# Attention with a gated MLP behind it on one core: the last 64 keys scored by four 64x64 fp32 products from the unsplit loads, and the attention's bursts aligned with pairs of units

## The chip, the cores and the metric

The kernel runs on one core of a Trainium2 chip. Its time is what the device reports for an execution, in microseconds (us), as the median over the runs. The engines are TensorE (PE for its matmuls, PEld for its weight loads), VectorE (DVE), ScalarE (ACT), GpSimd (POOL) and SyncE (SP), which here issues every transfer. Each engine runs its own instructions in the order of the program and waits for the others by semaphores.

## The reference

Eight batches, twelve heads, 448 positions, head width 64. Attention with a sigmoid in place of the softmax, and behind it a gated MLP in which the gate half is normalized and mixed over the positions:

```
scores = q @ k.T / sqrt(64) - log(448)
attn   = 1 / (1 + exp(-scores))
x      = heads side by side of (attn @ v)          # 8 x 448 x 768
h      = relu(x @ w_in);  u, g = halves of h       # 512 wide each
g      = (g - mean) / sqrt(var + 1e-6)             # over the 512
out    = (u * (w_spatial @ g + b_spatial)) @ w_out
```

Everything is fp32. Products run in two ways. In the **split** form both operands are cut in two fp32r parts, a high one (a rounded copy) and a low one (the rest), and three products are added: high-high, low-high, high-low (`TERMS`). In the **direct** form TensorE is given fp32 operands as they are; the trace then shows two matmul instructions for each.

## The kernel before

The work goes in four stages of two batches. A stage has attention for its two batches and then the MLP: `gate_values` (pv), `spatial` (pg), `gated` (pu), `output` (po). The MLP is not touched. A **unit** is two heads of one batch; its queries and keys lie in one load `raw`, 128 partitions by 896 columns, the two heads on partitions 0 to 63 and 64 to 127. Units are taken in pairs, six pairs to a stage, 24 in all.

448 keys are three tiles of 128 and a rest of 64. A pair of units makes seven score tiles (`TILES`): tiles 0 to 2 are the full ones of the first unit, tile 3 (`NFULL`) holds the last 64 keys of both units, one in the upper and one in the lower half of the partitions, tiles 4 to 6 are the full ones of the second unit.

- `attention_loads` (line 195) brings a unit's queries and keys, `value_loads` the values of a pair. Weight loads of the first stage share the buffers tagged `raw`, of which there are three.
- `attention_splits` (line 205) makes the two fp32r parts `qks` of a unit: a copy (ACT in the first stage, DVE later) and a subtraction on DVE (lines 99 and 100). A memset (line 212) puts 64 columns of zeros beside them. The keys of the first unit end with the 64-key rest and then the zeros; for the second unit the zeros and the rest stand in front. So a stationary operand of 128 columns, 64 of them zeros, can add one unit's rest to one half of tile 3.
- `attention_scores` (line 223): a full tile is three terms for each of two heads, six matmuls with 64 rows and 128 columns; the two heads use two row halves of TensorE and run at once. Tile 3 is twice that, twelve matmuls, six for each unit. The scores land in one of three two-bank buffers (`psc`); ACT turns them into `at` by the sigmoid (line 242), of which there are seven buffers.
- `attention_values` (line 247) multiplies `at` by the values, in direct fp32. A full tile is two products of 128 rows and 64 columns, one for each head, beside each other in TensorE's columns. Tile 3 is four products of 64 rows and 64 columns, in the four quadrants. The sums of a unit gather in one of two banks (`pav`), and when a unit is complete they are split into `x_s` (ACT copies, DVE subtracts).

The order on TensorE is the order of the program. The attention's tiles stand in one list, taken in **bursts of four** whatever unit they belong to: four score tiles, then the value products of the four before (`BURST`, lines 405 to 447). Loads and splits are issued from inside this loop, by the number of the tile. In the first stage, conversion of the weights (`load_weights`, mostly DVE work) runs between the tiles, one step for nearly every tile. The scores of the first three tiles of each later stage are put ahead of the last output products of the stage before.

Of the kernel before, what the change touches and what calls it, by code (L numbers as in the profile page):

```python
# [8 lines left out]
F32 = mybir.dt.float32  # L9
F32R = mybir.dt.float32r  # L10
U32 = mybir.dt.uint32
# [3 lines left out]
P = 128  # L15
# [20 lines left out]
def attn_gmlp_kernel(  # L36
# [25 lines left out]
    nc = tc.nc  # L62
    B, NHP, _, _ = qk.shape
    S = out.shape[3]
    D = P // 2
# [4 lines left out]
    HALF = 64  # L70
    NFULL = 3

    PART = 2 * S + HALF
    QK = 1.0 / math.sqrt(D)
    NEG_LOG_S = -math.log(S)
    NT = 2 * S // P
# [2 lines left out]
    work = ctx.enter_context(tc.tile_pool(name="work", bufs=2))  # L79
# [18 lines left out]
    def split(hi, lo, src, copy):  # L98
        copy(hi, src)  # L99
        nc.vector.tensor_sub(lo, src, hi.bitcast(F32))  # L100

    def banks(name):
        return ps_2.tile([P, 2, 512], F32, tag="ps2", name=name)
# [35 lines left out]
    def weight_steps():  # L139

        steps = []
        for i in range(NCC):
            steps += [(w_in, w_in_s, NCC + i)] + [(w_sp, w_sp_s, i)] * (i < NFC)
        steps += [(w_in, w_in_s, i) for i in range(NCC)]
        steps += [(w_out, w_out_s, i) for i in range(NFC * DM // 512)]
        raws = {}

        def load(n):
            if n < len(steps):
                src, _, i = steps[n]  # L150
                w = 512 if src is w_sp else 1024

                if n < NFIRST:
                    raw = work.tile([P, 1024], U32, tag="tmp", name=f"wraw_{n}", bufs=3)[:, :w]
                else:
                    raw = work.tile([P, 1024], U32, tag="raw", name=f"wraw_{n}", bufs=3)
                raws[n] = raw.bitcast(F32) if src is w_sp else raw
                nc.sync.dma_start(raws[n], src[:, i * w : (i + 1) * w])

        for n in range(AHEAD):  # L160
            load(n)
        for n, (src, dst, i) in enumerate(steps):
            load(n + AHEAD)
            if src is w_sp and i == 0:
                nc.sync.dma_start(b_bc, b_sp.broadcast_to([P, 512]))
            hi, lo = dst[:, i, 0], dst[:, i, 1]
            scalar = n >= NFIRST
            val = raws.pop(n)
            if src is not w_sp:
                raw = val  # L170
                val = work.tile([P, 512], U32, tag="wval", name=f"wval_{n}", bufs=2)
                yield from convert(val, raw, scalar)
                val = val.bitcast(F32)
            if scalar:
                nc.scalar.copy(hi, val)
                yield
            else:
                nc.vector.tensor_copy(hi, val)
            nc.vector.tensor_sub(lo, val, hi.bitcast(F32))
            if not scalar:  # L180
                yield


    NFIRST = NCC + NFC + 3

    weights = weight_steps()

    def load_weights(n):
        for _ in range(n):
            next(weights, None)  # L190

    loaded = {}
    values = {}

    def attention_loads(b, hp):
        raw = work.tile([P, 1024], F32, tag="raw", name=f"raw_{b}_{hp}", bufs=3)[:, : 2 * S]
        nc.sync.dma_start(raw, qk[b, hp])
        loaded[b, hp] = raw

    def value_loads(b, hp):  # L200
        vt = work.tile([P, 2 * NFULL + 1, P], F32, tag="v", name=f"v_{b}_{hp}", bufs=3)
        nc.sync.dma_start(vt, v[b, hp // 2])
        values[b, hp] = vt

    def attention_splits(b, hp):
        raw = loaded[b, hp]
        s = work.tile([P, 2, PART], F32R, tag="split", name=f"qks_{b}_{hp}", bufs=3)


        odd = hp % 2  # L210
        zeros = s[:, :, :HALF] if odd else s[:, :, 2 * S :]
        nc.vector.memset(zeros.bitcast(F32), 0.0)
        body = s[:, :, HALF:] if odd else s[:, :, : 2 * S]

        split(body[:, 0], body[:, 1], raw, nc.vector.tensor_copy if b > 1 else nc.scalar.copy)
        loaded[b, hp] = s

    TERMS = ((0, 0), (1, 0), (0, 1))


    TILES = 2 * NFULL + 1

    def attention_scores(b, hp, t):
        psc = banks(f"psc_{b}_{hp}_{t}")
        parts = []
        for odd in range(2):
            if t == NFULL or (t > NFULL) == odd:
                full = 2 * HALF if odd else 0
                k = (0 if odd else 2 * S - HALF) if t == NFULL else full + t % (NFULL + 1) * P
                parts += [(loaded[b, hp + odd], k, full + NFULL * P, a, e) for a, e in TERMS]  # L230
        for i, (s, k, q, a, e) in enumerate(parts):
            for j in range(2):
                rows = slice(j * D, (j + 1) * D)
                nc.tensor.matmul(  # L234
                    psc[:, j, :S],
                    s[rows, a, k : k + P],
                    s[rows, e, q : q + S],
                    start=i == 0,
                    stop=i == len(parts) - 1,
                )  # L240
        at = work.tile([P, 2, 512], F32, tag="big", name=f"at_{b}_{hp}_{t}", bufs=7)[:, :, :S]
        nc.scalar.activation(at, psc[:, :, :S], AF.Sigmoid, bias=bias_s, scale=QK)  # L242
        return at
# [3 lines left out]
    def attention_values(b, hp, t, at):  # L247
        vt = values[b, hp]
        for odd in range(2):
            if t == NFULL:  # L250
                rows = slice(odd * HALF, (odd + 1) * HALF)
            elif (t > NFULL) == odd:
                rows = slice(0, P)
            else:
                continue
            unit = b, hp + odd
            start = t == odd * NFULL
            stop = t == (1 + odd) * NFULL
            if start:
                pav_of[unit] = ps_1.tile([P, 512], F32, tag="ps1", name=f"pav_{b}_{hp + odd}")  # L260
            pav = pav_of[unit]
            for j in range(2):
                heads = slice(j * D, (j + 1) * D)
                nc.tensor.matmul(pav[heads, :S], vt[rows, t, heads], at[rows, j], start=start, stop=stop)  # L264
# [140 lines left out]
    BURST = 4  # L405
    units = [(b, hp) for b in range(B) for hp in range(NHP)]

    def ahead(f, n):
        if n < len(units):
            f(*units[n])  # L410

    def start_loads(m):
        n = m * 2 * NHP
        ahead(attention_loads, n)
        ahead(value_loads, n)
        ahead(attention_loads, n + 1)
        ahead(attention_loads, n + 2)

    def attention(m):

        first, end = 2 * NHP * m, 2 * NHP * (m + 1)
        tiles = [(n, t) for n in range(first, end, 2) for t in range(TILES)]
        before = []

        for i in range(-1, len(tiles) + BURST, BURST):
            now = []
            for n, t in tiles[max(i, 0) : i + BURST]:
                if n == first and t < 2:
                    ahead(attention_splits, n + t)
                if n + 2 < end:  # L430
                    if t == 0:
                        ahead(attention_loads, n + 3)
                        ahead(value_loads, n + 2)
                    elif t == NFULL and n + 4 < end:
                        ahead(attention_loads, n + 4)

                    elif t in (2, 5):
                        ahead(attention_splits, n + 2 + t // 5)
                now.append((*units[n], t, attention_scores(*units[n], t)))

                if m == 0 and i >= BURST - 1 and t != 2:
                    load_weights(1)
            yield
            for args in before:
                attention_values(*args)
            before = now
            yield
# [88 lines left out]
```

## Time and profile before

| what | value |
|---|---|
| median of 3 runs | 712.94 us (712.74 to 713.23) |
| profiled execution, first to last instruction | 711.3 us (the profile gives no other time of it) |
| PE busy | 696.7 us, 98% |
| DVE busy | 290.9 us, 41% |
| ACT busy | 256.2 us, 36% |
| score matmuls (line 234) | 1152, busy 137.3 us |
| value matmuls (line 264) | 768, busy 140.8 us |
| sigmoids (line 242) | 168, 1.007 us each |
| granted TensorE clock | 1.00 throughout |

How to read the views: a row of the timeline has the start and the length in us, the engine, the line, the operation, output<-inputs, the shapes and the number of instructions merged into the row; in brackets stands how long the engine was idle before it and what ended that. Shapes such as 64*128 are rows by columns of TensorE. A row of the groups has busy us and mean ns of one behind the bar, then the idle time before. A matmul's end is modelled, so durations of single matmuls overlap; the distance between the starts of two bursts is the safer measure. A row of the windows view has the stretch, its length, then the busy time and instruction count of PE, PEld, DVE, ACT and POOL, the granted clock, the share of time that the DMA engines were busy, and GB/s.

### The profile page before, as it was taken

How to read it: one execution, taken by the hardware profiler on the slowest of the kernel's cores; microseconds unless marked ns; L12 is line 12 of the kernel's file. 1: busy time of each engine (PE TensorE's matmuls, PEld its weight loads, DVE VectorE, ACT ScalarE, POOL GpSimd, SP SyncE). 2: the span in 40 equal slices, each digit the busy share in tenths (PEclk: the TensorE clock that was granted, in tenths of full speed). 3: DMA queues.
4: the chain of work that ended last, by engine and by line, in shares of the span. 5: the costliest groups of instructions: out<-in, count | busy, mean ns of one | idle time of the engine just before them, and what ended most of it. 6: DMA issues, size and time to landing. Idle time of an engine off the chain costs nothing.

```text
span 711.3 us, 9237 instructions
## 1 busy us (share of the span) xinstructions
PE 696.7 (98%) x3928; PEld 521.4 (73%) x3928; DVE 290.9 (41%) x494; ACT 256.2 (36%) x304; POOL 18.5 (3%) x36
## 2 busy tenths in 40 slices
PE   6999999999999999999999999999999999999997
PEld 4455688888755568999865548899986555889996
DVE  3999288723334226320234413722125331462110
ACT  6787221322477611001357661101136664101111
POOL 0000001000000001000000000100000000110000
PEclk9999999999999999999999999999999999999999
DMA  7773002320633200002253220000125310000102
GB/s 254 260 267 114 30 30 80 117 105 0 214 124 130 78 1 0 1 1 78 76 183 116 93 78 1 0 1 27 52 100 186 104 53 1 1 0 1 53 26 79
DMA packets 20249, 55.39 MB, mean 78 GB/s; under 512 B 1904, under 2 KB 8048, under 8 KB 20208
## 3 DMA queue, kind: packets, MB, share of 16 engines
q1 hardware_dynamic: 20208, 54.80, 22.6%
q8 instruction: 31, 0.51, 0.3%
q14 instruction: 10, 0.08, 0.0%
HBM read 43.78 MB, written 11.01 MB: 77 GB/s over the span
## 4 chain that ended last, share of the span: by engine, by line
PE 85%; DVE 9%; ACT 2%; issue 1%; DMA 1%; POOL 1%; SPq 0%; ACTq 0%
PE pav L264 19%; PE psc L234 17%; PE po L275 15%; PE pu L275 14%; PE pv L275 13%; PE pg L275 8%; DVE wval L128 1%; DVE g L374 1%; DVE vn L316 1%; ACT gs L99 1%; DVE wval L131 1%; ACT wraw L121 1%; DVE gs L100 1%; DMA wraw<-w_in_dram 1%; DVE stats L299 1%
## 5 line engine op out<-in xcount | busy, mean ns | idle before, releaser
L242 ACT ACTIVATE at<-psc,bias_s 128x896 f32<-128x896 f32 x168 | 160.3, 1007 | 53.9 <-PE psc L234 43.3
L234 PE MATMUL psc<-qks 64*128 64x448 f32 x1152 | 137.3, 379 | 6.0 <-ACT qks L99 4.8
L264 PE MATMUL pav<-at,v 128*64 128x448 f32 (+1 forms) x768 | 140.8, 552 | 0.7 <-DVE x_s L100 0.7
L234 PEld LDWEIGHTS psc<-qks 64*128 64x128 f32 x1152 | 104.2, 187 | 50.2 <-ACT x_s L99 17.6
L275 PE MATMUL po<-gs,w_out_s 128*128 128x448 f32 x576 | 122.1, 369 | 2.5 <-DVE gs L100 1.6
L275 PE MATMUL pu<-x_s,w_in_s 128*128 128x448 f32 x576 | 118.2, 365 | 1.0 <-DVE g L352 1.0
L275 PEld LDWEIGHTS po<-gs,w_out_s 128*128 128x128 f32 x576 | 107.2, 188 | 15.9 <-DVE gs L100 3.5
L275 PE MATMUL pv<-w_in_s,x_s 128*128 128x512 f32 x504 | 115.4, 390 | 0.0
L275 PEld LDWEIGHTS pu<-x_s,w_in_s 128*128 128x128 f32 x576 | 108.1, 188 | 9.9 <-DVE g L352 1.3
L275 PEld LDWEIGHTS pv<-w_in_s,x_s 128*128 128x128 f32 x504 | 94.3, 188 | 22.3 <-issue 2.8
L264 PEld LDWEIGHTS pav<-at,v 128*64 128x64 f32 (+1 forms) x768 | 41.7, 135 | 81.2 <-issue 79.1
L100 DVE TENSOR_TENSOR x_s<-pav,x_s 128x448 fp32r<-128x448 f32 x48 | 29.8, 623 | 115.6 <-ACT x_s L99 115.6
L275 PE MATMUL pg<-w_sp_s,vn 128*128 128x448 f32 x352 | 72.8, 365 | 0.0
L275 PEld LDWEIGHTS pg<-w_sp_s,vn 128*128 128x128 f32 x352 | 66.0, 187 | 5.8
L374 DVE SCALAR_TENSOR_TENSOR g<-pu,g 128x896 f32<-128x896 f32 x16 | 17.5, 1091 | 126.2 <-PE pu L275 126.2
L402 ACT COPY osb<-po 128x896 f32<-128x896 f32 x24 | 21.8, 907 | 113.0 <-PE po L275 113.0
L99 ACT CAST gs<-g 128x896 fp32r<-128x896 f32 x16 | 15.1, 943 | 129.8 <-DVE g L374 129.8
L100 DVE TENSOR_TENSOR qks<-raw,qks 128x896 fp32r<-128x896 f32 x48 | 51.9, 1081 | 8.4 <-ACT qks L99 7.2
L295 ACT ACTIVATE rv<-pv 128x1024 f32<-128x1024 f32 (+1 forms) x16 | 14.6, 914 | 83.5 <-PE pv L275 83.5
L299 DVE BATCH_NORM_STATS2 stats<-rv 128x6 f32<-128x512 f32 x28 | 19.0, 679 | 44.9 <-ACT rv L295 44.9
L99 ACT CAST x_s<-pav 128x448 fp32r<-128x448 f32 x48 | 25.5, 530 | 29.5 <-PE pav L264 29.5
L352 DVE TENSOR_TENSOR g<-pg,b_bc 128x896 f32<-128x896 f32 x16 | 17.4, 1088 | 20.0 <-PE pg L275 20.0
(32 smaller groups left out, 210.6 us busy)
## 6 DMA issues: line engine op xcount, KB each, us to landing
raw<-qk_dram SPq DMA_DIRECT2D x48, 448.0 KB, 4.1
v<-v_dram SPq DMA_DIRECT2D x24, 448.0 KB, 3.9
out_dram<-osb SPq DMA_DIRECT2D x24, 448.0 KB, 2.6
wraw<-w_in_dram SPq DMA_DIRECT2D x12, 512.0 KB, 4.3
wraw<-w_out_dram SPq DMA_DIRECT2D x6, 512.0 KB, 3.6
wraw<-w_sp_dram SPq DMA_DIRECT2D x4, 256.0 KB, 4.5
b_bc<-b_sp_dram SPq DMA_DIRECT2D x1, 256.0 KB, 4.7
```

The costliest lines, as they stand in the source:

```text
L99: copy(hi, src)
L100: nc.vector.tensor_sub(lo, src, hi.bitcast(F32))
L121: nc.scalar.mul(af, af, 2.0**-112)
L234: nc.tensor.matmul(psc[:, j, :S], s[rows, a, k : k + P], s[rows, e, q : q + S], start=i == 0, stop=i == len(parts) - 1,)
L242: nc.scalar.activation(at, psc[:, :, :S], AF.Sigmoid, bias=bias_s, scale=QK)
L264: nc.tensor.matmul(pav[heads, :S], vt[rows, t, heads], at[rows, j], start=start, stop=stop)
L275: nc.tensor.matmul(ps, st, mv, start=start and i == 0, stop=stop and i == len(ops) - 1)
L295: nc.scalar.activation(rv[:, :n], pv[:, :n], AF.Relu)
L299: nc.vector.bn_stats(stats, rv[:, i])
L352: nc.vector.tensor_add(g, pg[:, :, :S], bb)
L374: nc.vector.scalar_tensor_tensor(g, pu[:, :, :S], 0.0, g, op0=ALU.max, op1=ALU.mult)
L402: nc.scalar.copy(osb, po[:, :, :S])
```

## The change

Tile 3's scores are no longer made from the split parts. Four fp32 products with 64 rows and 64 columns read the keys' rest and the queries straight from `raw`, for two units and two heads, each in its own quadrant of TensorE. The zeros and their memset go, `qks` holds 832 columns in place of 896 (the rest's keys are not split), and the host lays out both units alike. `raw` stays in use until tile 3's scores, and has four buffers instead of three; `wval`, a buffer of the weights' conversion, has one instead of two. The order of loads at a stage's start becomes unit, unit, values, unit.

The order of the attention is written out by pairs of units: scores of tiles 0 to 2 and tile 3, values of the last four tiles of the pair before, scores of tiles 4 to 6, values of tiles 0 to 2. The second unit's split is now issued at tile 1 of its own pair, the next pair's first split at tile 4.

```diff
-    PART = 2 * S + HALF
+    REST = NFULL * P
+    PART = REST + S
...
-        zeros = s[:, :, :HALF] if odd else s[:, :, 2 * S :]
-        nc.vector.memset(zeros.bitcast(F32), 0.0)
-        body = s[:, :, HALF:] if odd else s[:, :, : 2 * S]
-
-        split(body[:, 0], body[:, 1], raw, nc.vector.tensor_copy if b > 1 else nc.scalar.copy)
-        loaded[b, hp] = s
+        split(s[:, 0], s[:, 1], raw[:, :PART], nc.vector.tensor_copy if b > 1 else nc.scalar.copy)
+        parts_of[b, hp] = s
...
+        heads = [slice(j * D, (j + 1) * D) for j in range(2)]
+        if t == NFULL:
+            for odd in range(2):
+                raw = loaded[b, hp + odd]
+                for j, rows in enumerate(heads):
+                    nc.tensor.matmul(
+                        psc[odd * HALF : (odd + 1) * HALF, j, :S],
+                        raw[rows, PART : PART + HALF],
+                        raw[rows, REST:PART],
+                        start=True,
+                        stop=True,
+                    )
+        else:
+            s = parts_of[b, hp + t // (NFULL + 1)]
+            k = t % (NFULL + 1) * P
+            for i, (a, e) in enumerate(TERMS):
+                for j, rows in enumerate(heads):
+                    nc.tensor.matmul(
+                        psc[:, j, :S],
+                        s[rows, a, k : k + P],
+                        s[rows, e, REST:PART],
+                        start=i == 0,
+                        stop=i == len(TERMS) - 1,
+                    )
...
+        def scores(n, tiles):
+            for t in tiles:
+                if t == 1 or n == first and t == 0:
                     ahead(attention_splits, n + t)
+                if n + 2 < end and t == NFULL + 1:
+                    ahead(attention_splits, n + 2)
+                waiting.append((*units[n], t, attention_scores(*units[n], t)))
                 if n + 2 < end:
                     if t == 0:
                         ahead(attention_loads, n + 3)
                         ahead(value_loads, n + 2)
                     elif t == NFULL and n + 4 < end:
                         ahead(attention_loads, n + 4)
...
+        for n in range(first, end, 2):
+            scores(n, range(NFULL))
+            if n == first:
+                yield
+            scores(n, [NFULL])
+            if n > first:
+                sums(NFULL + 1)
+            scores(n, range(NFULL + 1, TILES))
+            sums(NFULL)
+        sums(NFULL + 1)
```

`sums(k)` issues the value products of the k oldest tiles that wait for them.

TensorE's order around the third pair of the first batch, before. In the names, `psc_4_1` and `at_4_1` are tile 1 of the pair that begins with unit 4, `qks_4` and `raw_4` belong to unit 4, `pav_4` is its sum, `v_4` its values; the last number only counts buffers.

```order
L234 MATMUL psc_4_0_327<-qks_4_233 128x448 x6
L264 MATMUL pav_2_338<-at_2_0_214,v_2_92 64x448 x2
L264 MATMUL pav_2_338<-at_2_1_229,v_2_92 64x448 x2
L264 MATMUL pav_2_338<-at_2_2_244,v_2_92 64x448 x2
L264 MATMUL pav_2_338<-at_2_3_261,v_2_92 64x448 x2
L264 MATMUL pav_3_347<-at_2_3_261,v_2_92 64x448 x2
L234 MATMUL psc_4_1_352<-qks_4_233 128x448 x6
L234 MATMUL psc_4_2_369<-qks_4_233 128x448 x6
L234 MATMUL psc_4_3_380<-qks_4_233 128x448 x6
L234 MATMUL psc_4_3_380<-qks_5_293 128x448 x6
L234 MATMUL psc_4_4_401<-qks_5_293 128x448 x6
L264 MATMUL pav_3_347<-at_2_4_287,v_2_92 64x448 x2
```

The same place with the change:

```order
L239 MATMUL psc_4_0_305<-qks_4_256 128x448 x6
L239 MATMUL psc_4_1_323<-qks_4_256 128x448 x6
L239 MATMUL psc_4_2_336<-qks_4_256 128x448 x6
L227 MATMUL psc_4_3_345<-raw_4_130 64x448 x2
L227 MATMUL psc_4_3_345<-raw_5_197 64x448 x2
L269 MATMUL pav_2_298<-at_2_3_235,v_2_100 64x448 x2
L269 MATMUL pav_3_362<-at_2_3_235,v_2_100 64x448 x2
L269 MATMUL pav_3_362<-at_2_4_266,v_2_100 64x448 x2
L269 MATMUL pav_3_362<-at_2_5_279,v_2_100 64x448 x2
L269 MATMUL pav_3_362<-at_2_6_294,v_2_100 64x448 x2
L239 MATMUL psc_4_4_378<-qks_5_320 128x448 x6
L239 MATMUL psc_4_5_389<-qks_5_320 128x448 x6
```

The 64-key scores stand directly before the 64-key values of the pair before; a burst no longer cuts through a pair.

VectorE's order at the start of the program, before (`wraw` and `wval` belong to the first weight's conversion):

```order
L212 MEMSET qks_0_86 128x2x64
L100 TENSOR_TENSOR qks_0_86<-raw_0_78,qks_0_86 128x896
L212 MEMSET qks_1_103 128x2x64
L100 TENSOR_TENSOR qks_1_103<-raw_1_82,qks_1_103 128x896
L212 MEMSET qks_2_116 128x2x64
L100 TENSOR_TENSOR qks_2_116<-raw_2_84,qks_2_116 128x896
L112 TENSOR_SCALAR wval_152<-wraw_146 128x512
L123 TENSOR_SCALAR wraw_146<-wraw_146 128x512
L126 TENSOR_SCALAR wraw_146<-wraw_146 128x512
L128 SCALAR_TENSOR_TENSOR wval_152<-wraw_146,wval_152 128x512
```

And with the change:

```order
L101 TENSOR_TENSOR qks_0_86<-raw_0_78,qks_0_86 128x832
L101 TENSOR_TENSOR qks_1_102<-raw_1_80,qks_1_102 128x832
L113 TENSOR_SCALAR wval_138<-wraw_132 128x512
L124 TENSOR_SCALAR wraw_132<-wraw_132 128x512
L127 TENSOR_SCALAR wraw_132<-wraw_132 128x512
L101 TENSOR_TENSOR qks_2_142<-raw_2_84,qks_2_142 128x832
L129 SCALAR_TENSOR_TENSOR wval_138<-wraw_132,wval_138 128x512
```

The third unit's split has moved behind the first three instructions of the weight's conversion. On SP the order of these loads stays: raw_4, then the first weight.

More of the change, by code (lines that the diff above doesn't have):

```diff
@@ L155, in load @@
                 else:
-                    raw = work.tile([P, 1024], U32, tag="raw", name=f"wraw_{n}", bufs=3)
+                    raw = work.tile([P, 1024], U32, tag="raw", name=f"wraw_{n}", bufs=4)
                 raws[n] = raw.bitcast(F32) if src is w_sp else raw
@@ L170, in weight_steps @@
                 raw = val
-                val = work.tile([P, 512], U32, tag="wval", name=f"wval_{n}", bufs=2)
+                val = work.tile([P, 512], U32, tag="wval", name=f"wval_{n}", bufs=1)
                 yield from convert(val, raw, scalar)
@@ L195, in attention_loads @@
     def attention_loads(b, hp):
-        raw = work.tile([P, 1024], F32, tag="raw", name=f"raw_{b}_{hp}", bufs=3)[:, : 2 * S]
+        raw = work.tile([P, 1024], F32, tag="raw", name=f"raw_{b}_{hp}", bufs=4)[:, : 2 * S]
         nc.sync.dma_start(raw, qk[b, hp])
@@ L203, in value_loads @@
         values[b, hp] = vt
+    parts_of = {}
     def attention_splits(b, hp):
@@ L207, in attention_splits @@
         s = work.tile([P, 2, PART], F32R, tag="split", name=f"qks_{b}_{hp}", bufs=3)
-        odd = hp % 2
-        zeros = s[:, :, :HALF] if odd else s[:, :, 2 * S :]
-        nc.vector.memset(zeros.bitcast(F32), 0.0)
-        body = s[:, :, HALF:] if odd else s[:, :, : 2 * S]
-        split(body[:, 0], body[:, 1], raw, nc.vector.tensor_copy if b > 1 else nc.scalar.copy)
-        loaded[b, hp] = s
+        split(s[:, 0], s[:, 1], raw[:, :PART], nc.vector.tensor_copy if b > 1 else nc.scalar.copy)
+        parts_of[b, hp] = s
     TERMS = ((0, 0), (1, 0), (0, 1))
@@ L224, in attention_scores @@
         psc = banks(f"psc_{b}_{hp}_{t}")
[L225 to L240, printed above, removed]
+        heads = [slice(j * D, (j + 1) * D) for j in range(2)]
[22 more added lines that the diff above has]
+                    )
         at = work.tile([P, 2, 512], F32, tag="big", name=f"at_{b}_{hp}_{t}", bufs=7)[:, :, :S]
@@ L403, in output @@
         nc.sync.dma_start(out[b, es[0] : es[0] + 2].rearrange("e p s -> p e s"), osb)
-    BURST = 4
     units = [(b, hp) for b in range(B) for hp in range(NHP)]
@@ L414, in start_loads @@
         ahead(attention_loads, n)
+        ahead(attention_loads, n + 1)
         ahead(value_loads, n)
-        ahead(attention_loads, n + 1)
         ahead(attention_loads, n + 2)
@@ L421, in attention @@
         first, end = 2 * NHP * m, 2 * NHP * (m + 1)
[L422 to L428, printed above, removed]
+        waiting = []
+        def scores(n, tiles):
+            for t in tiles:
+                if t == 1 or n == first and t == 0:
                     ahead(attention_splits, n + t)
+                if n + 2 < end and t == NFULL + 1:
+                    ahead(attention_splits, n + 2)
+                waiting.append((*units[n], t, attention_scores(*units[n], t)))
                 if n + 2 < end:
@@ L435, in attention, with sums @@
                         ahead(attention_loads, n + 4)
[L437 to L441, printed above, removed]
+                if m == 0 and (n > first or t >= NFULL) and t != 2:
                     load_weights(1)
-            yield
-            for args in before:
+        def sums(n):
+            for args in waiting[:n]:
                 attention_values(*args)
-            before = now
-            yield
+            del waiting[:n]
+        for n in range(first, end, 2):
[8 more added lines that the diff above has]
+        sums(NFULL + 1)
     start_loads(0)
@@ L499 @@
     qk = np.concatenate([full, q, short], axis=2)
-    qk[:, 2::4] = np.concatenate([short, full, q], axis=2)[:, 2::4]
-    qk[:, 3::4] = np.concatenate([short, full, q], axis=2)[:, 3::4]
     qk = np.ascontiguousarray(np.transpose(qk, (0, 1, 3, 2))).reshape(B, H // 2, 2 * D, 2 * S)
```

## The prediction

> **What bounds the kernel now.** I read the page first: busy shares and the chain that ended last.
>
> ```profile
> span 711.3 us, 9237 instructions
> PE 696.7 (98%) x3928; PEld 521.4 (73%) x3928; DVE 290.9 (41%) x494; ACT 256.2 (36%) x304; POOL 18.5 (3%) x36
> PE 85%; DVE 9%; ACT 2%; issue 1%; DMA 1%; POOL 1%; SPq 0%; ACTq 0%
> PE pav L264 19%; PE psc L234 17%; PE po L275 15%; PE pu L275 14%; PE pv L275 13%; PE pg L275 8%; DVE wval L128 1%; DVE g L374 1%; DVE vn L316 1%; ACT gs L99 1%; DVE wval L131 1%; ACT wraw L121 1%; DVE gs L100 1%; DMA wraw<-w_in_dram 1%; DVE stats L299 1%
> ```
>
> TensorE sets the end. Lines 234 (scores) and 264 (values), which the change touches, hold 36% of the chain. A shorter PE stream there shortens the run, unless something else takes over. Next, the timeline of PE through the attention of the second stage (start, length, then the burst):
>
> ```profile
> 188.05 3.50 PE L234 MATMUL psc<-qks 64*128 64x448 f32 x30
> 191.48 2.48 PE L264 MATMUL pav<-at,v 128*64 128x448 f32 x12
> 193.88 3.54 PE L234 MATMUL psc<-qks 64*128 64x448 f32 x30
> 197.36 3.39 PE L264 MATMUL pav<-at,v 64*64 64x448 f32 x20
> ...
> 238.90 3.52 PE L234 MATMUL psc<-qks 64*128 64x448 f32 x30
> 242.35 3.39 PE L264 MATMUL pav<-at,v 64*64 64x448 f32 x20
> 245.67 2.08 PE L234 MATMUL psc<-qks 64*128 64x448 f32 x18
> 247.68 5.79 PE L264 MATMUL pav<-at,v 128*64 128x448 f32 x32
> 253.41 16.84 PE L275 MATMUL pv<-w_in_s,x_s 128*128 128x512 f32 x73
> ```
>
> Distances between starts are what the bursts cost. Three value tiles take 193.88 - 191.48 = 2.40 us; the last seven, with the 64-key tile among them, 253.41 - 247.68 = 5.73. With a for a value tile (four instructions, or eight 64x64 ones) and c for a change of tile shape, 3a + c = 2.40 and 7a + 3c = 5.73 are both met by a = 0.75, c = 0.16. A burst of three score tiles (18 matmuls, nine concurrent pairs) takes 247.68 - 245.67 = 2.01: less c, 1.85, or 0.206 per pair. Closer, one burst of each kind:
>
> ```profile
> 225.96 2.92 PE L234 MATMUL psc<-qks 64*128 64x448 f32 x24
> 226.94 3.95 ACT L242 ACTIVATE at<-psc,bias_s 128x896 f32<-128x896 f32 x4 [1.63 <-PE psc L234]
> ...
> 228.00 0.50 PEld L234 LDWEIGHTS psc<-qks 64*128 64x128 f32 x6 [0.33 <-ACT at L242]
> ...
> 228.80 3.54 PE L264 MATMUL pav<-at,v 128*64 128x448 f32 x20
> 229.71 0.21 PEld L264 LDWEIGHTS pav<-at,v 64*64 64x64 f32 x8 [0.70 <-issue]
> 230.62 0.20 PEld L264 LDWEIGHTS pav<-at,v 128*64 128x64 f32 x4 [0.71 <-issue]
> ```
>
> Two things. The 64-key value tile holds PE for 230.62 - 229.71 = 0.91 = a + c: four fp32 64x64 products cost one a. And the fourth score tile of a burst begins at 228.00, 2.04 after the burst, where three tiles need 1.85: it waits for the first tile's sigmoid, since there are three score buffers. Four pairs of units, in the windows view (us, then PE, PEld, DVE, ACT busy):
>
> ```profile
> 193.88:238.90 45.02, 45.02 (x322) 24.00 (x320) 18.16 (x31) 30.64 (x36) 0.00 (x0) 1.00 0.36 121
> ```
>
> 45.02 / 4 = 11.26 us per pair of units. Built from the pieces: 24 concurrent score pairs x 0.206 = 4.93, seven value tiles x 0.75 = 5.25, five changes of shape x 0.16 = 0.80, together 10.98; the remaining 0.28 are stalls on that fourth tile. ACT is busy 30.64 and DVE 18.16 of 45.02, so neither is near here, and the granted clock is 1.00.
>
> **The change in the steady pairs.** It removes twelve matmuls (six concurrent pairs) per pair of units: 6 x 0.206 = -1.23. It adds four fp32 64x64 products. No row has these operands; the nearest is the value tile of the same shape, and I take its a = +0.75. Each row group writes a bank of its own in both cases. Below 0.75 nothing speaks: all four quadrants are used already. Above it stand 1.50 (two at a time) and 3.0 (one after another), treated as rivals. Shape changes stay five: scores, 64x64, values, scores, values, scores, because the 64-key scores stand directly before the previous pair's 64-key values. Bursts of three need no fourth buffer, so the 0.28 goes; but the 64-key scores are a fourth tile behind three. They can begin 2.04 after the burst's start and would without a wait at 1.85 + 0.16 = 2.01, so the wait is 0.03 if the change of shape runs beside it and up to 0.2 if it comes after. I take 0.1. A steady pair is then 18 x 0.206 + 0.75 + 5.25 + 0.80 + 0.1 = 10.60 against 11.26.
>
> Stages two to four, from 188.05 to 253.41 = 65.36 before: first pair 0.91 + 2.01 + 2.40 = 5.3 (its first three tiles were scored earlier, as now), five pairs of 10.60 = 53.0, last four value tiles 4 x 0.75 + 2 x 0.16 = 3.3. Sum 61.6, gain 3.7 a stage (4.2 with no wait, 3.1 with 0.22), three stages 11.1 (9.3 to 12.6).
>
> **Edits that I cost at nothing.** In these stages ACT has 14 us of 45 free and DVE 27, which covers the splits moved to tiles 1 and 4: the second needs a copy and a subtraction behind the sums' last x_s, and PE reads it three score and three value tiles later, 2.01 + 2.41 = 4.4 us.
>
> ```profile
> L99 DVE CAST qks<-raw 128x896 fp32r<-128x896 f32 x36 | 20.5, 569 | 5.4 <-DMA raw<-qk_dram 5.4
> ```
>
> With the subtraction's 1.03 and an x_s of 0.62 (both rows below) that is 2.2 behind ACT's copy of the sums: over 1 us to spare, and only what exceeds 4.4 would cost. The raw loads now wait for the 64-key product instead of the split.
>
> ```profile
> raw<-qk_dram SPq DMA_DIRECT2D x48, 448.0 KB, 4.1
> ```
>
> A load issued behind the product of pair n is split a full pair later, over 10 us on, against 4.1. The single wval buffer adds no wait: on DVE the next conversion already stands behind the subtraction of the last, which needs ACT's copy of it. Removed memsets cost PE nothing here.
>
> **The first stage** differs: weights are converted between the tiles.
>
> ```profile
> 20.00:30.00 10.00, 9.31 (x66) 4.05 (x64) 9.73 (x20) 6.96 (x9) 0.00 (x0) 1.00 0.80 258
> ...
> 40.00:50.00 10.00, 10.00 (x72) 4.97 (x70) 9.69 (x20) 7.94 (x10) 0.00 (x0) 1.00 0.95 332
> ```
>
> DVE is busy 97% there: 10.9 us of each 11.26. Its groups in 20 to 60 us:
>
> ```profile
> L100 DVE TENSOR_TENSOR qks<-raw,qks 128x896 fp32r<-128x896 f32 x7 | 7.2, 1028 | 0.0
> L179 DVE TENSOR_TENSOR w_in_s<-wval,w_in_s 128x512 fp32r<-128x512 f32 x7 | 4.8, 693 | 0.2
> L100 DVE TENSOR_TENSOR x_s<-pav,x_s 128x448 fp32r<-128x448 f32 x7 | 4.2, 616 | 0.0
> L131 DVE SCALAR_TENSOR_TENSOR wval<-wraw,wval 128x512 uint32<-128x512 uint32 x6 | 4.2, 692 | 0.2
> L126 DVE TENSOR_SCALAR wraw<-wraw 128x512 f32<-128x512 f32 x7 | 3.1, 437 | 0.2
> L178 DVE CAST w_in_s<-wval 128x512 fp32r<-128x512 f32 x6 | 2.5, 418 | 0.0
> L212 DVE MEMSET qks<- 128x128 f32 x7 | 1.2, 165 | 0.0
> ```
>
> Per pair of units two memsets go (0.33), and two subtractions shrink from 896 to 832 columns (2 x 0.07): DVE needs 10.4, PE 10.6. DVE just keeps up, with no room. And at the start it now has the third split behind the first weight's conversion:
>
> ```profile
> 7.09 1.01 ACT L242 ACTIVATE at<-psc,bias_s 128x896 f32<-128x896 f32 x1 [2.34 <-PE psc L234]
> 7.99 0.93 ACT L99 CAST qks<-raw 128x896 fp32r<-128x896 f32 x1
> ...
> 10.07 0.33 SPq L197 DMA_DIRECT2D raw<-qk_dram  x1
> 10.44 0.43 SPq L158 DMA_DIRECT2D wraw<-w_in_dram  x1
> ...
> 15.49 0.43 DVE L112 TENSOR_SCALAR wval<-wraw 128x512 uint32<-128x512 uint32 x1 [3.71 <-DMA wraw<-w_in_dram]
> ...
> 26.98 3.39 PE L264 MATMUL pav<-at,v 128*64 128x448 f32 x20 [0.69 <-DVE x_s L100]
> ```
>
> The fifth raw load, ahead of the weight on SP, now waits for the first 64-key product. That product needs the first sigmoid's buffer (7.09 + 1.01 = 8.1) and 0.9 more, so the two loads are issued at 9.2 and 9.6; with the 5.05 us from 10.44 to 15.49 the weight is there at 14.65. Three conversions (3 x 0.44) and the subtraction (1.03 for 896 columns in the rows above, so 0.96 for 832) end at 17.0. PE has run out by then: the seventh score tile needs the buffer of the fourth sigmoid, so behind the first one a split copy (0.9) and three sigmoids (3.95 for four, above: 0.96 apart) to 11.9; it ends at 12.5 and three value tiles at 14.9. PE stands for 2.1 us. From 17.0: 2.01 + 0.75 + 3.32 end the first four-tile sums at 23.1 and three score tiles at 25.1. DVE meanwhile does 2 x 0.69 + 0.42 + 0.69 (weight), 0.42 + 0.69 (spatial weight), 3 x 0.44, a subtraction of 0.96, and 2 x 0.69 + 0.42 + 0.69 again: 8.4, to 25.4, then x_s 0.62, to 26.0. The next value product needs the bank that this frees: 0.9 more of a stall. From 26.0: 2.41 + 4 x 10.60 + 3.32 = 74.1.
>
> ```profile
> 76.90 28.86 PE L275 MATMUL pv<-w_in_s,x_s 128*128 128x512 f32 x126
> ```
>
> The first stage's attention ended at 76.90, so it gains 2.8; nothing if DVE falls behind, 4.2 as elsewhere if the weight lands early enough. The rest of each stage stays as it is.
>
> **Sum:** 11.1 + 2.8 = 13.9, from the profiled span of 711.3 to 697.4. The median of the runs, 712.94, lies 1.6 above that span (launch and end, unchanged): 699.0.
>
> **Rivals.** *VectorE takes the first stage.* For it: 97% busy, and in-order waits on x_s with weight work behind them. Against: its work falls by 0.48 per pair, PE's by 0.66. Then that stage gains nothing: 712.94 - 11.1 = 701.8, and 703.6 with the long wait at the 64-key tile.
>
> *The four quadrants share out badly: slower.* The four score products come in another order than the value products: both units' row groups first, then the second column group. If the latter two wait for the first two, the tile costs 1.50, every pair of units 0.75 more, 24 x 0.75 = 18.0 - 13.9: 4.1 slower, 717.0. One after another, 3.0 and 24 x 2.25 - 13.9 = 40 slower, 753. It decides above 0.75 + 13.9 / 24 = 1.33 us for the tile. Against it, in the windows view, the value tile that began at 65.84:
>
> ```profile
> 65.94:66.04 0.10, 0.10 (x4) 0.10 (x8) 1.00 0.00 0
> ```
>
> Four matmuls run at once, and eight weight loads beside them. [...]
>
> *The loads come late*, since raw buffers are held longer: a load would have to take over 10 us instead of 4.1 to 5.05; I give it no case of its own.
>
> **How the numbers follow.** Forecast 0.70, VectorE in the first stage 0.19, the quadrants 0.07 (two turns 0.05, four 0.02), something better than 695.5 or not thought of 0.04. The forecast's own ends are 12.6 + 4.2 (696.1) and 9.3 + 2.8 (700.8); the range goes on through the first rival: 695.5 to 704. A measurement tells about 0.2%, 1.4 us, from no change: faster 0.92, the same 0.02, slower 0.06.
>
> **What would show it.** Right: PE's bursts in stages two to four start 10.5 to 10.7 us apart per pair; the 64x64 scores and the 64x64 values behind them hold PE 1.6 to 1.9 together; no three-tile burst waits on ACT; in the first stage PE waits for the split of the third unit near 15 to 17 us, and its attention ends near 74. Wrong: a 64-key score tile of 1.5 us or more, waits of PE on DVE in each pair of the first stage, or waits on raw loads.

## The result, and the profile after

The changed kernel takes 700.76 us (four runs, 699.55 to 700.91) against 712.84 (712.70 to 713.23): ratio 0.9825, 95% interval 0.9811 to 0.9839, 12 us less. The prediction was 699.0 in a range of 695.5 to 704. Two runs of the experiments below, of 964.88 and 1726.77 us, lie far outside all others and are left out of their medians. The page of the profile after:

```profile
span 699.1 us, 9084 instructions
PE 683.1 (98%) x3832; PEld 504.5 (72%) x3832; DVE 283.2 (41%) x446; ACT 253.9 (36%) x304; POOL 18.5 (3%) x36
PE 87%; DVE 7%; ACT 2%; issue 2%; DMA 1%; POOL 1%; SPq 0%; ACTq 0%
```

TensorE still sets the end. Its timeline through the second stage's attention:

```profile
187.59 0.98 PE L227 MATMUL psc<-raw 64*64 64x448 f32 x8
188.50 2.11 PE L239 MATMUL psc<-qks 64*128 64x448 f32 x18
190.54 2.48 PE L269 MATMUL pav<-at,v 128*64 128x448 f32 x12
192.95 2.09 PE L239 MATMUL psc<-qks 64*128 64x448 f32 x18
194.99 0.98 PE L227 MATMUL psc<-raw 64*64 64x448 f32 x8
195.79 3.34 PE L269 MATMUL pav<-at,v 64*64 64x448 f32 x20
199.06 2.09 PE L239 MATMUL psc<-qks 64*128 64x448 f32 x18
...
203.48 2.09 PE L239 MATMUL psc<-qks 64*128 64x448 f32 x18
...
243.21 5.79 PE L269 MATMUL pav<-at,v 128*64 128x448 f32 x32
248.94 11.41 PE L280 MATMUL pv<-w_in_s,x_s 128*128 128x512 f32 x49
```

The 64-key scores hold PE for 195.79 - 194.99 = 0.80 us, with no change of shape to the 64x64 values behind them. A pair of units takes 203.48 - 192.95 = 10.53 (11.26 before), the stretch 248.94 - 187.59 = 61.35 (65.36). Stages three and four give 61.63 (418.88 - 357.25) and 61.34 (588.53 - 527.19), where the kernel before has 65.34 in both, so the three stages gained 11.7 together.

The first stage is different. PE's timeline, and then the windows view of the same time (the granted clock is the third number from the end):

```profile
9.12 1.77 PE L227 MATMUL psc<-raw 64*64 64x448 f32 x8
10.82 2.25 PE L239 MATMUL psc<-qks 64*128 64x448 f32 x18
...
15.40 0.47 PE L239 MATMUL psc<-qks 64*128 64x448 f32 x2
17.93 3.36 PE L239 MATMUL psc<-qks 64*128 64x448 f32 x16 [2.06 <-DVE qks L101]
21.21 1.03 PE L227 MATMUL psc<-raw 64*64 64x448 f32 x8
...
75.21 28.88 PE L280 MATMUL pv<-w_in_s,x_s 128*128 128x512 f32 x126
```

```profile
16.00:18.00 2.00, 0.07 (x2) 0.07 (x2) 1.93 (x5) 0.00 (x0) 0.00 (x0) 0.99 0.51 209
18.00:20.00 2.00, 2.00 (x12) 1.80 (x14) 1.90 (x4) 0.85 (x1) 0.00 (x0) 0.50 0.00 0
20.00:21.00 1.00, 1.00 (x8) 0.63 (x4) 0.96 (x3) 1.00 (x3) 0.00 (x0) 0.50 0.74 244
21.00:22.00 1.00, 1.00 (x10) 0.40 (x12) 0.97 (x3) 1.00 (x2) 0.00 (x0) 0.82 0.54 174
```

PE idled 2.06 us for the third unit's split, as predicted. Unpredicted is what came behind: the clock was granted at 0.50, and the sixteen score matmuls from 17.93 to 21.21 took 3.28 us. The attention ended at 75.21 against 76.90, 1.7 less. And the first stage's MLP got longer, from 76.90 to the next scores at 175.95 before (99.05), from 75.21 to 175.49 now (100.28). Its two waits of PE, before and after:

```profile
123.10 7.57 PE L275 MATMUL pu<-x_s,w_in_s 128*128 128x448 f32 x36 [0.98 <-DVE g L352]
...
145.72 10.12 PE L275 MATMUL po<-gs,w_out_s 128*128 128x448 f32 x48 [0.86 <-DVE g L352]
```

```profile
121.85 7.57 PE L280 MATMUL pu<-x_s,w_in_s 128*128 128x448 f32 x36 [1.39 <-DVE g L357]
...
144.96 10.12 PE L280 MATMUL po<-gs,w_out_s 128*128 128x448 f32 x48 [1.00 <-DVE g L357]
```

So the span's 12.2 us are 11.7 in stages two to four, 1.7 in the first attention, and 1.2 given back in the first MLP, 0.55 of it in these waits.

### The profile page after: what moved, and what is told of

Read it like the earlier page. It is cut to its first block, busy times and chain, and to the rows that moved or that the text cites. A ratio compares the mean times of both kernels' runs of the same rounds, so it can differ in the third digit from the quotient of the medians.

```text
span 699.1 us, 9084 instructions
## 1 busy us (share of the span) xinstructions
PE 683.1 (98%) x3832; PEld 504.5 (72%) x3832; DVE 283.2 (41%) x446; ACT 253.9 (36%) x304; POOL 18.5 (3%) x36
## 4 chain that ended last, share of the span: by engine, by line
PE 87%; DVE 7%; ACT 2%; issue 2%; DMA 1%; POOL 1%; SPq 0%; ACTq 0%
PE pav L269 19%; PE po L280 15%; PE pu L280 15%; PE psc L239 14%; PE pv L280 14%; PE pg L280 8%; PE psc L227 3%; DVE g L379 1%; ACT gs L100 1%; DVE wval L129 1%; DVE wval L132 1%; DVE gs L101 1%; ACT wraw L122 1%; DVE stats L304 1%; DMA wraw<-w_in_dram 1%
## 5 line engine op out<-in xcount | busy, mean ns | idle before, releaser
L269 PE MATMUL pav<-at,v 128*64 128x448 f32 (+1 forms) x768 | 139.4, 546 | 0.0
L239 PEld LDWEIGHTS psc<-qks 64*128 64x128 f32 x864 | 79.9, 190 | 45.7 <-ACT at L247 14.8
L239 PE MATMUL psc<-qks 64*128 64x448 f32 x864 | 104.4, 383 | 7.2 <-ACT qks L100 4.8
L269 PEld LDWEIGHTS pav<-at,v 128*64 128x64 f32 (+1 forms) x768 | 44.0, 135 | 80.6 <-issue 76.3
L101 DVE TENSOR_TENSOR qks<-raw,qks 128x832 fp32r<-128x832 f32 x48 | 49.2, 1024 | 8.2 <-ACT qks L100 6.9
L100 DVE CAST qks<-raw 128x832 fp32r<-128x832 f32 x36 | 21.1, 587 | 28.9 <-PE po L280 20.2
```

The source lines that it names most:

```text
L239: nc.tensor.matmul(psc[:, j, :S], s[rows, a, k : k + P], s[rows, e, REST:PART], start=i == 0, stop=i == len(TERMS) - 1,)
```

## The experiments

Theory at this point: the direct product and the order gain what the sum says; the order of VectorE's work at the start costs the idle stretch, the idle stretch costs the clock, and the single `wval` buffer costs the first MLP. Rivals: the gain is all from one of the two parts; VectorE bounds the first stage anyway; the clock falls for another reason.

**Only the direct product.** The changed kernel, with the old bursts of four and the old places of the splits:

```diff
-        for n in range(first, end, 2):
-            scores(n, range(NFULL))
...
+        tiles = [(n, t) for n in range(first, end, 2) for t in range(TILES)]
+        for i in range(-1, len(tiles) + BURST, BURST):
...
+                    elif t in (2, 5):
+                        ahead(attention_splits, n + 2 + t // 5)
+                now.append((*units[n], t, attention_scores(*units[n], t)))
+                if t == NFULL and n + 4 < end:
+                    ahead(attention_loads, n + 4)
```

> The changed kernel with the old order: bursts of four tiles that cut through the pairs, splits at tiles 2 and 5, the load of unit n+4 just behind tile 3's scores. Only the direct fp32 tile (and four raw buffers, one wval buffer) is left of the change. By the sum: per pair 18 x 0.206 + 0.75 + 5.25 + 0.80 = 10.50, plus 0.24 for six more changes of shape in four pairs (the 64x64 scores now stand inside score bursts), plus 0.17 for the wait on a fourth tile in three of seven bursts: 10.9 against 11.26 before and 10.53 of the changed kernel; stages two to four take 63.1 to 63.5 from the second score burst to the first pv product (65.36 before, 61.35 changed). With a first stage that doesn't idle for the third split: 702.5 to 705. If the direct product is the whole gain and the order nothing: 700.8. If the order is most of it: above 709.

Measured: 704.26 us, ratio to the kernel before 0.9871 (0.9852 to 0.9890). From its PE timeline in the second stage:

```profile
205.51 0.98 PE L227 MATMUL psc<-raw 64*64 64x448 f32 x8
206.42 0.88 PE L239 MATMUL psc<-qks 64*128 64x448 f32 x6
207.22 3.23 PE L269 MATMUL pav<-at,v 128*64 128x448 f32 x16
210.38 2.91 PE L239 MATMUL psc<-qks 64*128 64x448 f32 x24
213.22 3.54 PE L269 MATMUL pav<-at,v 128*64 128x448 f32 x20
```

Inside a score burst the 64x64 tile takes 206.42 - 205.51 = 0.91, a change of shape included, as against 0.80 beside the 64x64 values, where there is none; the burst of four full tiles keeps its wait (213.22 - 210.38 = 2.84 for 12 x 0.206 + 0.16 = 2.63 of work). Seven bursts, four pairs, from 191.82 to 235.45 take 43.63, 10.91 a pair; 10.9 was expected. Each of stages two to four takes 62.82 (186.48 to 249.30 in the second), a little less than the 63.1 to 63.5 expected. The direct product alone, with the buffers of the changed kernel, is worth about 8.7 us.

**Only the order.** The kernel before with the changed kernel's `attention` loop; tile 3 stays twelve matmuls from split parts.

```diff
-        for i in range(-1, len(tiles) + BURST, BURST):
...
+        for n in range(first, end, 2):
+            scores(n, range(NFULL))
...
+            scores(n, [NFULL])
+            if n > first:
+                sums(NFULL + 1)
+            scores(n, range(NFULL + 1, TILES))
+            sums(NFULL)
```

> The kernel before with the new order alone: scores 0 to 3, four value tiles, scores 4 to 6, three value tiles; tile 3 still made of twelve matmuls from split parts, three raw buffers, memsets kept. By the sum: steady pair 10.98 plus a wait of 0.19 on the fourth tile = 11.17 against 11.26, stages two to four 0.5 shorter each. In the first stage the third unit's split comes behind the first weight's conversion, as in the changed kernel: an idle stretch of PE of about 2 us near 16 us and, if the clock falls there too, 1.2 more. Total 712 to 714.5. If the order carries half of the gain or more: below 707.

Measured: 724.95 us, 1.0156 (1.0134 to 1.0177): far slower than either theory said. In the second stage a pair takes 215.45 - 204.26 = 11.19, as expected, and the stage 65.07 against 65.36, 0.3 less where 0.5 was expected. The first stage's attention ends at 87.25 instead of 76.90. PE's waits of this run:

```profile
PE psc L234 <- DVE qks L212: 4.8, 5, 2.4
PE psc L234 <- DVE qks L100: 3.9, 7, 1.8
```

and PE with DVE in the third pair:

```profile
35.47 0.69 DVE L179 TENSOR_TENSOR w_in_s<-wval,w_in_s 128x512 fp32r<-128x512 f32 x1
36.13 0.17 DVE L212 MEMSET qks<- 128x128 f32 x1
36.22 1.03 DVE L100 TENSOR_TENSOR qks<-raw,qks 128x896 fp32r<-128x896 f32 x1
36.45 0.47 PE L234 MATMUL psc<-qks 64*128 64x448 f32 x2 [0.53 <-DVE qks L212]
```

Tile 3 made from split parts needs the second unit's split. In the new order that split is issued at tile 1, and in the first stage VectorE reaches it only behind a weight's conversion, so PE waits in every pair from the second on.

**The order with the old places of the splits.** The same kernel with the splits at tiles 2 and 5 of the pair before:

```diff
-                if t == 1 or n == first and t == 0:
+                if n == first and t < 2:
                     ahead(attention_splits, n + t)
-                if n + 2 < end and t == NFULL + 1:
-                    ahead(attention_splits, n + 2)
+                if n + 2 < end and t in (2, 5):
+                    ahead(attention_splits, n + 2 + t // 5)
```

> The kernel before with the new order of tiles, as in the run that gave 724.95, but the splits where the kernel before has them: the next pair's units at tiles 2 and 5. Theory (that loss lay in the place of the splits: tile 3 from split parts needs the second unit one tile sooner, and in the first stage VectorE has no room): PE's waits on the splits go, the first stage's attention ends within 1 us of the 76.9 of the kernel before, stages two to four take 65.07 as in that run against 65.36, the time is 711.3 to 713.0. Rival (the order itself costs in the first stage): above 716.

Measured: 712.89 us, 0.9998 (0.9989 to 1.0008). PE's waits on the splits shrink from 8.7 to 0.4; it waits 1.5 once on the bank of the sums (0.7 in the kernel before), and the first attention ends at 76.94. So the 12 us lay in the place of the splits, and the order by itself is worth nothing that can be measured. With the direct product it is worth 3.5 (704.26 - 700.76). In stages two to four it gains 4.1 there (three times 62.82 against 61.35, 61.63 and 61.34), because it removes three of seven waits on a fourth tile and six changes of shape in four pairs. The late split of a pair's second unit costs PE nothing, because tile 3 no longer reads it; but the late split of the third unit makes the idle stretch of 2.06, and the first attention ends at 75.21 instead of 74.46 in the kernel with the direct product only.

**One wval buffer.** The kernel before with this line alone:

```diff
-                val = work.tile([P, 512], U32, tag="wval", name=f"wval_{n}", bufs=2)
+                val = work.tile([P, 512], U32, tag="wval", name=f"wval_{n}", bufs=1)
```

> The kernel before with one wval buffer instead of two, nothing else. As predicted (no added wait): the distance from the subtraction of a weight (line 179) to the next conversion's first instruction (line 112) stays at 0.60 us and the time at 712.8. By the theory formed from the changed kernel's trace (there it is 0.72): 0.12 more for each of 18 conversions, PE's two waits on the g of line 352 in the first stage's MLP grow from 0.98 and 0.86 to about 1.4 and 1.0, the time to 713.3 to 713.6.

Measured: 713.94 against 713.00, 1.0012 (1.0002 to 1.0022). DVE in the first MLP, the kernel before and then this one:

```profile
102.31 0.69 DVE L179 TENSOR_TENSOR w_in_s<-wval,w_in_s 128x512 fp32r<-128x512 f32 x1
102.92 0.42 DVE L112 TENSOR_SCALAR wval<-wraw 128x512 uint32<-128x512 uint32 x1
```

```profile
102.59 0.69 DVE L179 TENSOR_TENSOR w_in_s<-wval,w_in_s 128x512 fp32r<-128x512 f32 x1
103.31 0.43 DVE L112 TENSOR_SCALAR wval<-wraw 128x512 uint32<-128x512 uint32 x1
```

From start to start 0.61 became 0.72: with two buffers the next instruction begins before the last has ended, with one it waits for its end. PE's two waits in this run are 1.4 and 1.0, those of the changed kernel, and the stretch from the end of the first attention to the next scores takes 100.05 (77.06 to 177.11) instead of 99.05.

**The third split ahead of the weight.**

```diff
-                if n + 2 < end and t == NFULL + 1:
+                if n + 2 < end and t == NFULL + (n > 0):
                     ahead(attention_splits, n + 2)
```

> The changed kernel with one line different: in the first pair of a stage the next pair's first unit is split at tile 3 instead of tile 4, so in the first stage VectorE subtracts for the third unit before the first weight's conversion. Theory: PE's idle stretch of 2.06 us near 16 us goes, and the stretch at a granted clock of 0.50 behind it (1.2 us lost) goes with it; the attention of the first stage ends near 72 instead of 75.2, the time is 697.3 to 698.5. Rival, VectorE bounds the first stage: the wait only moves, to the bank of the sums or to a later split, and the time stays within 0.8 of 700.8.

Measured: 698.98 us, 0.9798 (0.9780 to 0.9817). The idle stretch is gone and the clock is 1.00 from 16 us on, but the first attention ends at 73.37, not 72. Its waits of PE:

```profile
PE pav L269 <- DVE x_s L101: 1.2, 1, 1.2
...
PE psc L239 <- ACT at L247: 0.8, 1, 0.8
```

Both theories hold in part: of about 3.3 us, 1.8 came off the end of this attention. Not all of the 1.8 need be the edit's: TensorE came up to speed sooner at the start of this profile (its first 64-key tile took 10.10 - 9.19 = 0.91 us instead of 1.70), and VectorE began the first weight at 15.09 instead of 15.59. The wait on the bank of the sums, which the prediction had put at 0.9, comes back once PE arrives on time.

**The idle stretch filled.** The changed kernel, and beside it the same with nine pairs of products in the idle stretch, whose results are overwritten:

```diff
+            if (b, hp, t) == (0, 2, 0):
+                other = parts_of[0, 1]
+                for _ in range(9):
+                    for j, rows in enumerate(heads):
+                        nc.tensor.matmul(
+                            psc[:, j, :S],
+                            other[rows, 0, :P],
+                            other[rows, 0, REST:PART],
+                            start=True,
+                            stop=True,
+                        )
```

> The changed kernel itself again, beside the next three on one chip: 700.8, with single runs near 699.5 where the granted clock does not fall behind the idle stretch near 16 us.

> The changed kernel with nine pairs of products more on TensorE: into the score bank of unit 2's tile 0, from the parts of unit 1, right behind the first three value tiles. Their result is overwritten by the scores that follow; they fill the 2.06 us in which TensorE idled for the third split, and change no wait. If the stretch at a granted clock of 0.50 behind the idle time is due to that idle time: the clock stays at 1.00 there, the six tiles' scores behind it take 2.0 instead of 3.3 us, the first stage's attention ends near 74.0 instead of 75.2 and the median is 699.4 to 699.8. If the clock falls anyhow (start of the run, direct fp32 products): 700.8, or up to 0.3 more.

Measured: 699.55 (699.16 to 700.71; ratio 0.9813, 0.9801 to 0.9826) without, 699.66 (0.9814, 0.9801 to 0.9827) with the products. The two profiles, without and with:

```profile
18.06 3.36 PE L239 MATMUL psc<-qks 64*128 64x448 f32 x16 [2.16 <-DVE qks L101]
21.35 1.01 PE L227 MATMUL psc<-raw 64*64 64x448 f32 x8
```

```profile
17.57 1.91 PE L250 MATMUL psc<-qks 64*128 64x448 f32 x16 [0.37 <-DVE qks L101]
19.42 0.98 PE L227 MATMUL psc<-raw 64*64 64x448 f32 x8
...
26.42 2.48 PE L280 MATMUL pav<-at,v 128*64 128x448 f32 x12 [0.84 <-DVE x_s L101]
```

With the stretch filled the clock stays at 1.00 and the same sixteen matmuls take 1.85 instead of 3.29; 0.84 of it goes to the wait on the bank of the sums, and the attention ends at 74.39 instead of 75.36. That gain of 0.97 is not the clock's alone. In the profile with the products TensorE also came up to speed sooner at the start (its first 64-key tile took 10.46 - 9.06 = 1.40 us, against 10.81 - 9.12 = 1.69), VectorE began the first weight at 15.23 instead of 15.72, and it came sooner to the subtractions that free the bank. They are, without and with the products:

```profile
26.22 1.15 DVE L101 TENSOR_TENSOR x_s<-pav,x_s 128x448 fp32r<-128x448 f32 x2
```

```profile
25.74 1.15 DVE L101 TENSOR_TENSOR x_s<-pav,x_s 128x448 fp32r<-128x448 f32 x2
```

With the products, the value products begin 0.68 behind the start of this row, at 26.42. The same 0.68 in the profile without them gives 26.90, and they began at 27.47. So the fall of the clock costs about 0.6 there, an estimate from these rows: of the 1.44 that the scores lost, the rest would have gone to the wait on the bank.

The medians don't differ, because the clock doesn't fall in every run. In the changed kernel's first profile the fall to 0.50 lasts 3.4 us (the windows view has 0.94 from 17.5 to 18, 0.50 from 18 to 21, 0.65 from 21 to 21.5, and 1.00 before and behind); that takes 3.4 x 0.5 / 699 = 0.0024 off the mean clock of a run. Of eight runs of the changed kernel, the three with a mean clock of 0.996 took 700.69 to 700.91, four with 0.998 to 1.000 took 699.16 to 699.65, and one with 1.000 took 700.83. So runs with the fall are about 1.2 us longer, with one exception; the two medians of the changed kernel lie as far apart. How much of the 1.2 is the fall itself, and how much a late start of the kind just seen, is open, since both runs with a trace have the fall. That the idle stretch brings the fall is shown by these profiles and by the mean clocks: of thirteen runs with the stretch (eight of the changed kernel, five of the next one) four have 0.996 or 0.997, and of thirteen without it (four with these products, five with the early split, four with both edits below) none is under 0.998.

**Clip first.** In the nine weights that ACT takes part in, the instruction that writes `wval` moves behind the clip:

```diff
-        nc.vector.tensor_scalar(l, a, 0x80000000, None, op0=ALU.bitwise_and)
+        def sign():
+            nc.vector.tensor_scalar(l, a, 0x80000000, None, op0=ALU.bitwise_and)
...
             nc.vector.tensor_scalar(af, af, -bound, bound, op0=ALU.max, op1=ALU.min)
+            sign()
             yield
```

> The changed kernel; where ACT shares in a weight's conversion (nine weights, from the end of the first attention on), VectorE clips first and takes the sign into wval after that, so the instruction that waits for wval no longer stands ahead of the one that ACT waits for, and it runs while ACT works. Theory (the single wval buffer and the hand-over to ACT bound the first stage's MLP): PE's waits of 1.39 and 1.00 on the g of line 357 go, 698.2 to 699.0. Rival (the g is late for other reasons): 700.4 to 701.

Measured: 699.09, 0.9800 (0.9788 to 0.9813), 0.5 below the changed kernel beside it, which the intervals don't separate. PE's two waits fall from 1.39 and 1.00 to 0.92 and 0.88, to about what they are with two buffers, and no further, and the first MLP takes 99.03 (75.55 to 174.58), against 99.96 of the changed kernel beside it (75.36 to 175.32) and 99.05 of the kernel before. The buffer's share is explained; what holds the remaining 0.9 of each wait is open.

**Both.** The early split and the clip first, the two edits above together:

> Both: the third unit split at tile 3 (as in the run that gave 698.98) and the clip first. If the two gains are independent: 698.98 - 2.0 to 2.4 = 696.6 to 697.0. If the MLP only shifts and the weights' transfers or VectorE's chain are bound to the start: 698 or more.

Measured: 697.98, 0.9789 (0.9776 to 0.9801), 1.0 below the early split alone, which was measured on another chip; by the ratios to the kernel before it is 0.6, and the intervals overlap. It has the lowest time here. The two waits of 0.9 stay.

**No weights in the first pair.** With both of these, four conversion steps leave the first pair of units and come later:

```diff
-                if m == 0 and (n > first or t >= NFULL) and t != 2:
+                if m == 0 and n > first and t != 2:
                     load_weights(1)
```

> The changed kernel with the third unit split at tile 3, the clip first, and no weight conversion in the first pair of units (four steps come later). Theory: the wait of 1.16 us on the bank of the sums, which VectorE's weight work causes near 25 us, goes too, and the time is 696.6 to 697.2. Rival: VectorE has no room later in the first stage, so the four steps come back as waits in its later pairs or its MLP: 698 to 700.

Measured: 701.49, 0.9838 (0.9821 to 0.9855). The first attention does end at 71.68, without the wait on the bank. Then the MLP waits for its weights:

```profile
PE po L284 <- ACT w_out_s L180: 3.0, 1, 3.0
...
PE pu L284 <- DVE w_in_s L184: 1.4, 1, 1.4
PE po L284 <- DVE w_out_s L184: 1.2, 2, 0.7
```

The rival was right in kind, and the time is above its 698 to 700: VectorE has no room in the first stage (busy 9.34 to 9.69 of every 10 us from 20 to 70), and what is put off there comes back with more. Behind the wait of 3.0 the matmuls slowed as well: the 34 po matmuls from 141.41 took 8.78 us, where in the changed kernel 48 take 10.12.

## Why the prediction was right, point by point

- **The 64-key tile, +0.75:** right. It takes 0.80 beside the 64x64 values, without a change of shape, and 0.91 with one (188.50 - 187.59). The groups view, in which the modelled ends overlap what follows, has 24.4 us for 24 of these tiles, and 22.6 for as many 64x64 value tiles:

```profile
L227 PE MATMUL psc<-raw 64*64 64x448 f32 x192 | 24.4, 580 | 0.2 <-ACT at L247 0.2
L269 PE MATMUL pav<-at,v 64*64 64x448 f32 x192 | 22.6, 540 | 0.0
```

  The rival of two turns (1.50) is out: its 1.50 was the author's estimate, twice the price of a value tile, and no run shows it. In their own order the four score products cost little more than a value tile, 0.80 against 0.75.
- **The wait on the fourth tile, 0.1:** too much. It is hidden beside the change of shape: 10.53 a pair is 10.51 + 0.02, the low end. Stages two to four gained 11.7 instead of 11.1; only one pair of eighteen had a wait of 0.23.
- **The order's part:** the prediction doesn't split its gain. Its pieces, added up for the direct product alone before that run, gave 10.9 a pair, and 10.91 was measured.
- **Edits costed at nothing in stages two to four:** right. PE has no wait on a split or a load there.
- **The first stage, 2.8:** the mechanism was right and the size off; 1.7. The first 64-key tile was expected to begin behind the first sigmoid, at 8.1, and to take 0.9. It began at 9.12, since the score tiles ahead of it ran at half speed (sixteen matmuls in 3.28 us, 1.85 later in the profile with the products), and took 1.70, where 0.91 is its price with a change of shape; so the loads behind it on SP went at 10.92 and 11.29 instead of 9.2 and 9.6. The weight's transfer was shorter (4.30 instead of 5.05): it landed at 15.59 instead of 14.65, and the split ended 0.9 late. PE ran out of work about 1 us late too, so the idle time came out at 2.06, near the forecast of 2.1, although both of its ends were off; that agreement is in part luck. From the split to the next pair's first value products took 9.42 (17.93 to 27.35) instead of 9.0: the scores took 3.28 at the lower clock instead of 2.01, and the wait of 0.9 on the bank, which was in the sum, did not come, because PE was late itself. The pairs behind gave 0.3 back, and the end was 75.21 instead of 74.1.
- **"The single wval buffer adds no wait":** wrong, the one step that failed outright. VectorE's order does put the next conversion behind the subtraction, but before it began 0.1 us ahead of that one's end, and with one buffer it can't. It costs 1.0 us of the first MLP of the kernel before (100.05 instead of 99.05, 0.6 of it in the two waits) and 0.9 (0.12%) in its time.
- **"The rest of each stage stays":** right in stage two (108.31 us from the end of the attention to the next 64-key or fourth tile, before and after). In the first MLP 1.2 was lost. 0.9 is the buffer's: the kernels with one buffer take 99.93 to 100.05 there, all but this profile, and those with two, or with the clip first, 99.03 to 99.10, the kernel with the late weights aside. The other 0.3 is one block of 72 pu matmuls that took 14.87 instead of 14.58; in the second profile of the changed kernel the same block takes 14.58 (155.04 to 169.62), so it does not belong to the change.
- **The sum, 13.9:** 12.2 was measured: 1.1 less in the first attention, 1.2 less in the first MLP, 0.6 more in stages two to four. The misses partly cancel.
- **The rival "VectorE takes the first stage":** half right. It did not stop the steady pairs, which run at 10.5 there too, but each attempt to give PE back its time at the start met VectorE again.

## What to carry to other kernels

Build the cost of a burst from differences of starts (so much per tile, so much per change of tile shape, so much per wait on a buffer), and check that the pieces give the measured period before changing one: here they gave 10.91 and 10.53 for two orders that the trace of before had not shown. Take a burst's price from rows at the speed that holds where it will stand: the first 64-key tile, priced at full speed, took nearly twice as long at the start. A new order of work has to be costed together with what each tile reads: the same order was worth -12, 0 or +3.5 us, by where the splits stood and whether tile 3 needed them. In a stretch where a helper engine is busy 97%, count what stands ahead of each moved instruction in its queue, and count a buffer taken away as the overlap of two neighbours lost (here 0.61 us from start to start became 0.72), even when the engine's order already serializes them.

## What the runs showed of the hardware that was not expected

- An idle stretch of 2.06 to 2.2 us brought the granted clock to 0.50 for 3.4 us, in some runs; waits of 0.8 to 1.4 us in the same profiles did not. In the profile of the order alone a wait of 1.83 that ended at 17.52 did not bring it (1.00 from 0 to 20 us), and one of 2.35 that ended at 22.58 did: the mean from 20 to 30 us is 0.83, as 3.4 us at 0.50 would make it, and the twenty value products at 24.48 took 4.09 instead of 3.32. In that of the late weights the matmuls slowed behind the wait of 2.96. Why the fall comes in some runs and not in others, and how long a wait has to be, these runs do not show.
- At the start of the changed kernel the matmuls run at half speed while the view of the windows shows 1.00: sixteen score matmuls took 3.28 us from 5.84 to 9.12, as long as at 0.50 later, and the first 64-key tile 1.70.

```profile
5.84 3.35 PE L239 MATMUL psc<-qks 64*128 64x448 f32 x16 [0.32 <-DVE qks L101]
```

How long this lasts differs between profiles: the first 64-key tile takes 1.70, 1.69, 1.40 and 0.91 us in those of the changed kernel, of its second measurement, with the products and with the early split. The kernel before starts slowly too, so the "1.00 throughout" of its table does not mean full speed in the first microseconds. Its windows view has 12 score matmuls in two busy microseconds at the start, and 20 later:

```profile
6.00:8.00 2.00, 2.00 (x12) 1.77 (x14) 0.01 (x1) 0.91 (x2) 0.00 (x0) 1.00 0.92 337
...
16.00:18.00 2.00, 2.00 (x20) 1.57 (x20) 1.90 (x4) 1.30 (x2) 0.00 (x0) 1.00 0.26 103
```
